# Moving the loads of three attention units inside a fused kernel

## The chip, the cores and the metric

The kernel runs on one core of one Trainium2 chip. The metric is the device time of one execution in microseconds (us). Before the change it is 703.27 us, the median of three runs (702.09 to 704.14).

## The reference

The reference is a chain of three blocks on a batch of 4, with 8 heads, 768 positions and a head size of 48:

```
f = sigmoid(f_logit)                                  # gated linear attention, token by token
state = f_t * state + k_t (outer) v_t ;  y_t = q_t . state
x = y, heads side by side                             # [4, 768, 384]
h = relu(x^T @ w_tok1) @ w_tok2 ; u = x + h^T         # mixer over tokens (256 hidden)
x2 = u + relu(u @ w_ch1) @ w_ch2                      # mixer over channels (1536 hidden)
h = relu(x2 @ w_in)                                   # gated feed-forward (1024 hidden)
out = (h * sigmoid(conv3(h))) @ w_out                 # conv of 3 taps along the sequence
```

Weights arrive as 64-bit floats.

## The kernel before, in words

The attention is cut into 16 **units**: unit u is one batch and one pair of heads, so units 0 to 3 are batch 0. A unit has four inputs, `f`, `k`, `q` (112 x 768 each) and `v` (128 x 6 x 96). `elem_steps(u)` turns the forget gates into decay factors: s1 to s3 on ScalarE (L385, L388, L391: exp, then log in two halves), s4 a running sum on VectorE (L396), s5 a small copy (L401) and exp on ScalarE (L403), s7 multiplies `k` by it (L410), s6 is another exp on ScalarE (L406) and s8 multiplies `q` by that (L414). For units 0 to 4 both products run on VectorE. Then TensorE transposes `k` (`T`), multiplies chunks of `q` and `k` (`A`), sums up states (`U`) and forms the output (`Y`). ScalarE copies their results out, L468 (`am`), L420 (`kn` and the states `S`), L521 (`xn`); GpSimd masks `am` (L469).

The weights are cut into 34 pieces (0 to 33). Each is loaded into a staging buffer (L318), decoded from 64-bit by three VectorE operations (L65, L67, L69) and split into a high part on ScalarE (L329) and a low part on VectorE (L330). The first 20 pieces have six staging buffers by turns; two decoded buffers exist, so a decode waits until the piece two before it is split.

The kernel has four stretches: the **front** (`first_gla`, units 0 to 3, with the decode of the first pieces woven in); then for each batch an MLP of token and channel mixer (`mlp_a`), into which the units of the next batch are woven (`gla_steps`, `merge`); last the gated feed-forward of all batches. The first MLP also decodes the late weight pieces.

What sets the order: every matrix multiplication, every first operation of a decode (L65) and the steps of units 1 and 4 to 15 are kept in the order of the code. All else (DMA issues on the queue of SyncE, ScalarE, the rest of VectorE) is put in order by a planner that runs a timeline of its own: at each moment an engine is given, of the instructions that its model holds ready, the one that stands first in the code. An instruction is ready when its inputs are there and its buffer has been given up by the last reader. The order is then fixed; on the chip every engine works through its list and waits at the head of it.

Loads are issued in SyncE's queue by `load_unit(u)` (f, k, q) and `load_v(u)`. Their buffers: `f` one (tag "f", pool `gl`), but units 1 and 3 share another ("r10", pool `pa`); `k` two; `q` three, but unit 3 takes one of the four buffers "xhl" that later hold the split of x; `v` two. In the code, step u of the front ends with the loads of unit u+2 (`load_unit(u + 2)`, `load_v(u + 2)`), and so do the steps in `gla_steps`. `zipl` weaves two lists evenly.

Of the kernel before, what the change touches and what calls it, by code (L numbers as in the profile page):

```python
# [8 lines left out]
F32 = mybir.dt.float32  # L9
# [9 lines left out]
B, H, S, D = 4, 8, 768, 48  # L19
DM = H * D  # L20
NP_ = H // 2
P = 128
DT_TOK, D_CH, D_FF = 256, 1536, 1024
HR = 112
# [196 lines left out]
def chunked_path(ctx, tc, psum, flags, qT, kT, fT, vN, w_tok1, w_tok2, w_ch1, w_ch2, w_in, conv_w, w_out, outT):  # L221
    nc = tc.nc
# [42 lines left out]
    pa = ctx.enter_context(tc.tile_pool(name="pa", bufs=1))  # L265
    gl = sa.enter_context(tc.tile_pool(name="gl", bufs=2))

    units = [(b, p) for b in range(B) for p in range(NP_)]
    st = [dict() for _ in units]

    def load_unit(u, between=(lambda: None,) * 3):
        b, p = units[u]
        d = st[u]
        pool, tag = (pa, "r10") if u in (1, 3) else (gl, "f")
        d["f"] = pool.tile([HR, S], F32, tag=tag, name=f"f{u}", bufs=1)
        d["k"] = gl.tile([HR, S], F32, tag="k", name=f"k{u}")
        if u == 3:
            d["q"] = pa.tile([HR, S], F32, tag="xhl", name=f"q{u}", bufs=4)
        else:
            d["q"] = gl.tile([HR, S], F32, tag="q", name=f"q{u}", bufs=3)  # L280
        for i, (n, src) in enumerate((("f", fT), ("k", kT), ("q", qT))):
            nc.sync.dma_start(out=d[n], in_=src[b, p])
            between[i]()

    def load_v(u):
        b, p = units[u]
        st[u]["v"] = gl.tile([P, NC_, 2 * D], F32, tag="v", name=f"v{u}")
        nc.sync.dma_start(out=st[u]["v"], in_=vN[b, p])
# [21 lines left out]
    def weight_piece(dst, src, n, shape, pool, stage=("wst", 3)):  # L310

        cols = shape[0] * (shape[1] if len(shape) > 1 else 1)
        box = {}

        def load():
            box["s"] = pool.tile([P, cols], I64, tag=stage[0], name=f"wst{n}", bufs=stage[1])
            o = box["s"]
            nc.sync.dma_start(out=o if len(shape) == 1 else o.rearrange("p (a b) -> p a b", a=shape[0]), in_=src)  # L318

        def dec():  # L320
            box["w"] = pool.tile([P, cols], U32, tag="wdc", name=f"wdc{n}", bufs=2)

            decode_f64(nc, box["w"], box["s"], tc.keep_in_program_order)
            w = box["w"].bitcast(F32)
            box["w"] = w if len(shape) == 1 else w.rearrange("p (a b) -> p a b", a=shape[0])

        def split():
            ready.add(n)
            nc.scalar.activation(dst[0], box["w"], AF.Copy)  # L329
            (nc.vector if isinstance(n, int) else nc.gpsimd).tensor_tensor(  # L330
                out=dst[1], in0=box["w"], in1=dst[0].bitcast(F32), op=ALU.subtract)

        return [load, dec, split]

    def pipelined(pieces, lead=1):
        res = []
        n = len(pieces)
        for i in range(n + lead + 1):
            g = []
            if 0 <= i - lead < n:  # L340
                g.append(pieces[i - lead][1])
            if 0 <= i - lead - 1 < n:
                g.append(pieces[i - lead - 1][2])
            if i < n:
                g.append(pieces[i][0])
            res.append(g)
        return res
# [17 lines left out]
    first = [f for g in wgroups[:LEAD] for f in g]  # L365
    wgroups = wgroups[LEAD:]
    first[0]()
    load_unit(1, (first[1], lambda: load_v(0), first[2]))
    wlate = pipelined([weight_piece(d, sr, NDEEP + n, sh, pa) for n, (d, sr, sh) in enumerate(wpieces[NDEEP:])], LATE)

    def conv_weights():
# [7 lines left out]
    def elem_steps(u):  # L379
        d = st[u]  # L380

        pin = tc.keep_in_program_order if u >= NP_ or u == 1 else lambda ins: ins

        def s1():
            pin(nc.scalar.activation(d["f"], d["f"], AF.Exp, scale=-1.0, accum_out=SE[:, u:u + 1]))  # L385

        def s2():
            pin(nc.scalar.activation(d["f"][:, :HS], d["f"][:, :HS], AF.Ln, bias=1.0, accum_out=T1[:, u:u + 1]))  # L388

        def s3():  # L390
            pin(nc.scalar.activation(d["f"][:, HS:], d["f"][:, HS:], AF.Ln, bias=1.0))  # L391

        def s4():
            pool, tag = (pa, "r11") if u in (1, 3) else (gl, "c")
            d["c"] = pool.tile([HR, S], F32, tag=tag, name=f"c{u}", bufs=1)
            (pin if u != 1 else lambda ins: ins)(nc.vector.tensor_tensor_scan(d["c"], zcol[:HR].to_broadcast([HR, S]), d["f"], T1[:, u:u + 1],  # L396
                                                                 op0=ALU.add, op1=ALU.subtract))

        def s5():

            pin(nc.vector.tensor_scalar(out=T2[:, u:u + 1], in0=d["c"][:, S - 1:S], scalar1=-1.0, scalar2=None,  # L401
                                        op0=ALU.mult))
            pin(nc.scalar.activation(d["f"], d["c"], AF.Exp, scale=-1.0))  # L403

        def s6():
            pin(nc.scalar.activation(d["c"], d["c"], AF.Exp))  # L406

        def s7():
            eng = nc.vector if KE[min(u, 5)] == "v" else nc.gpsimd
            eng.tensor_tensor(out=d["k"], in0=d["k"], in1=d["f"], op=ALU.mult)  # L410

        def s8():
            eng = nc.vector if QE[min(u, 5)] == "v" else nc.gpsimd
            eng.tensor_tensor(out=d["q"], in0=d["q"], in1=d["c"], op=ALU.mult)  # L414

        return [s1, s2, s3, s4, s5, s7, s6, s8]
# [13 lines left out]
    def pm(*a, **k):  # L430

        tc.keep_in_program_order(mm(*a, **k))  # L432
# [93 lines left out]
    def new_x(b):  # L526
        xn[b] = pa.tile([P, NC_, DM], F32, tag="xn", name=f"xn{b}", bufs=2)

    def first_gla(wb):

        def keep_busy(u):

            for _ in range(NBUSY[u]):
                pm(wb[:, :256], lhsT=wz[:, :P], rhs=wz, start=True, stop=True)

        e = elem_steps(1)
        parts = [elem_steps(0) + e[:3] + [lambda: load_v(1), lambda: new_x(0)]]
        for u in range(NP_ + 1):
            ahead, products = [], []
            if u + 1 < NP_:  # L540
                ahead = elem_steps(u + 1) if u else e[3:]
                if u + 2 < NP_ + 1:
                    ahead += [lambda u=u: load_unit(u + 2), lambda u=u: load_v(u + 2)]
            if u < NP_:
                products += [lambda u=u: T(u), lambda u=u: A(u, 0), lambda u=u: A(u, 1)]
            if u:
                products += [lambda u=u: Y(u - 1, 0), lambda u=u: Y(u - 1, 1)]
            if u < NP_:
                products += [lambda u=u: U(u)]
            parts.append(zipl([joined(f, lambda u=u: keep_busy(u)) for f in products], ahead))  # L550
        return sum(parts[:4], []), sum(parts[4:], [])

    def gla_steps(b):

        u0, n = b * NP_, (b + 1) * NP_
        steps = []
        for u in range(u0 if b == 1 else u0 + 1, n + 1):
            new = u < len(units)
            s = []
            if new:  # L560
                s.append([lambda u=u: T(u)])
            s.append([lambda u=u: A(u, 0)] * new + [lambda u=u: Y(u - 1, 0)] * (u > u0))
            s.append([lambda u=u: A(u, 1)] * new + [lambda u=u: Y(u - 1, 1)] * (u > u0))
            if b == 1 and u == u0:

                s.append([])
            s[-1] += [lambda u=u: U(u)] * new
            ahead = []
            if u + 1 < len(units):
                ahead = elem_steps(u + 1)  # L570
            if u + 2 < len(units):
                ahead += [lambda u=u: load_unit(u + 2), lambda u=u: load_v(u + 2)]
            if u + 1 == n and n < len(units):
                ahead = [lambda: new_x(b + 1)] + ahead

            cuts = [0, 4, 7 if b == 1 else 6] if len(s) > 2 else [0, 4]
            for i, blk in enumerate(s):
                steps.append(joined(*blk))
                steps += ahead[cuts[min(i, len(cuts) - 1)] if i < len(cuts) else len(ahead):
                               cuts[i + 1] if i + 1 < len(cuts) else len(ahead)]  # L580
        return steps

    def joined(*fs):
        return lambda: [f() for f in fs]
# [298 lines left out]
    for i in range(len(seq) + 2):  # L883
        if i < len(seq):
            b, ff = seq[i]
# [6 lines left out]
            for _ in range(min(len(wsteps), 2)):  # L892
                f = wsteps.pop(0)
# [54 lines left out]
```

## Time and profile before

| | |
|---|---|
| median of 3 runs | 703.27 us |
| the profiled execution's own time | 702.62 us |
| its span, first to last instruction | 700.9 us |
| PE busy | 680.8 us (97%) |
| DVE (VectorE) busy | 407.0 us (58%) |
| ACT (ScalarE) busy | 292.1 us (42%) |
| POOL (GpSimd) busy | 116.5 us (17%) |
| moved by DMA | 55.19 MB |

The span is counted from the first to the last instruction. The engines' shares are means over stretches with different limits: TensorE is nearly always busy after the front, while in the front, the first 57.5 us, several engines and the DMA engines have their turns as the limit.

### The profile page before, as it was taken

The numbers are of one execution on the slowest core, as the hardware profiler recorded it, in microseconds if no ns is written. First come the engines' busy times: TensorE is split into PE (matmuls) and PEld (weight loads), VectorE is DVE, ScalarE is ACT, GpSimd is POOL, SyncE is SP. The second block draws the span as 40 slices with busy tenths as digits, with TensorE's granted clock in tenths as the row PEclk, the third lists the DMA queues.
The fourth block names the chain that finished last, engine by engine and source line by source line (L and its number), as shares of the span: only waits on it lengthen the run. The fifth ranks groups of instructions, "written<-read, shape, count | busy, mean of one in ns | idle before, by whom it ended". The sixth has DMA issues, their size and how long they took to land.

```text
span 700.9 us, 12681 instructions
## 1 busy us (share of the span) xinstructions
PE 680.8 (97%) x5228; PEld 651.8 (93%) x5228; DVE 407.0 (58%) x719; ACT 292.1 (42%) x613; POOL 116.5 (17%) x96
## 2 busy tenths in 40 slices
PE   7898999999999999999999999999999999999995
PEld 5678998999999999999999999999999999999995
DVE  6799995554334432143342154384677968876774
ACT  6665355554433342233234132242444544444432
POOL 2340002234112113011112022332303004000000
PEclk9979999999999999999999999999999999999999
DMA  9995453244022302002001021240301200100102
GB/s 238 267 265 163 141 177 93 78 119 112 35 77 77 91 21 77 35 20 59 35 19 68 20 83 69 79 158 23 102 0 49 88 1 0 68 1 1 68 0 73
DMA packets 26114, 55.19 MB, mean 79 GB/s; under 512 B 2880, under 2 KB 12096, under 8 KB 26048
## 3 DMA queue, kind: packets, MB, share of 16 engines
q1 hardware_dynamic: 22448, 49.38, 23.9%
q10 hardware_dynamic: 3600, 4.92, 2.0%
q8 instruction: 43, 0.70, 0.4%
q14 instruction: 23, 0.19, 0.1%
HBM read 44.85 MB, written 9.44 MB: 77 GB/s over the span
## 4 chain that ended last, share of the span: by engine, by line
PE 79%; DVE 7%; DMA 6%; issue 3%; ACT 2%; POOL 1%; SPq 0%; ACTq 0%; POOLq 0%; DVEq 0%
PE acc L432 22%; PE c L432 19%; PE h L844 14%; PE o L866 13%; PE Y L432 4%; PE t L432 4%; DMA f<-in_fT_dram 4%; PE A L432 3%; DVE wdc L67 1%; DMA wst<-in_w_tok_dram 1%; DVE wdc L69 1%; DMA x2d<-xo 1%; DVE wdc L65 1%; DVE c L396 1%; DVE wc L330 1%
## 5 line engine op out<-in xcount | busy, mean ns | idle before, releaser
L432 PE MATMUL c<-u,wc 128*128 128x384 f32 x864 | 169.4, 339 | 0.8 <-ACT u L671 0.4
L432 PE MATMUL acc<-hid,wc 128*128 128x384 f32 x864 | 164.6, 336 | 0.0
L432 PEld LDWEIGHTS c<-u,wc 128*128 128x128 f32 x864 | 149.5, 188 | 5.7 <-DVE u L672 1.6
L432 PEld LDWEIGHTS acc<-hid,wc 128*128 128x128 f32 x864 | 150.5, 188 | 0.5
L646 DVE SCALAR_TENSOR_TENSOR hid<-c,hid 128x384 fp32r<-128x384 f32 x96 | 53.4, 556 | 135.7 <-ACT hid L645 135.4
L844 PE MATMUL h<-x2r,wi 128*128 128x384 f32 (+2 forms) x576 | 108.9, 338 | 0.1
L866 PE MATMUL o<-gbuf,wo 128*128 128x384 f32 x576 | 105.8, 335 | 0.0
L844 PEld LDWEIGHTS h<-x2r,wi 128*128 128x128 f32 x576 | 101.6, 188 | 0.4 <-ACT hp L846 0.4
L866 PEld LDWEIGHTS o<-gbuf,wo 128*128 128x128 f32 x576 | 100.5, 188 | 0.4 <-ACT gbuf L827 0.4
L645 ACT ACTIVATE hid<-c 128x384 fp32r<-128x384 f32 x96 | 47.0, 490 | 118.2 <-PE c L432 117.8
L823 DVE SCALAR_TENSOR_TENSOR cv<-hp,cwu,cv 128x768 f32<-128x768 f32 (+1 forms) x66 | 69.8, 1058 | 1.2
L825 ACT ACTIVATE cv<-cv 128x768 f32<-128x768 f32 (+1 forms) x33 | 27.3, 827 | 69.2 <-DVE cv L823 69.0
L410 POOL TENSOR_TENSOR k<-k,f 112x768 f32<-112x768 f32 x11 | 20.1, 1826 | 181.7 <-ACT f L403 101.0
L826 DVE TENSOR_TENSOR cv<-cv,hp 128x768 f32<-128x768 f32 (+1 forms) x33 | 32.5, 983 | 25.5 <-ACT cv L825 25.4
L846 ACT ACTIVATE hp<-h 128x384 f32<-128x384 f32 (+1 forms) x64 | 30.6, 485 | 26.7 <-PE h L844 26.5
L784 POOL TENSOR_TENSOR x2r<-x,x2r 128x768 fp32r<-128x768 f32 x12 | 24.7, 2080 | 94.8 <-ACT x2r L783 86.2
L828 DVE TENSOR_TENSOR gbuf<-cv,gbuf 128x768 fp32r<-128x768 f32 (+1 forms) x33 | 32.3, 979 | 5.4 <-ACT gbuf L827 5.3
L396 DVE TENSOR_TENSOR_SCAN c<-zcol,T,f 112x768 f32<-112x768 f32 x16 | 29.0, 1813 | 9.5 <-ACT f L391 9.5
L432 PEld LDWEIGHTS A<-q,k 48*128 48x128 f32 x384 | 25.7, 194 | 9.5 <-issue 5.5
L432 PE MATMUL A<-q,k 48*128 48x128 f32 x384 | 32.4, 298 | 1.2 <-DVE am L472 0.4
L827 ACT ACTIVATE gbuf<-cv 128x768 fp32r<-128x768 f32 (+1 forms) x33 | 27.2, 823 | 15.2 <-DVE cv L826 12.6
L821 DVE TENSOR_SCALAR cv<-hp,cwu 128x768 f32<-128x768 f32 (+1 forms) x33 | 23.1, 699 | 15.7 <-ACT hp L846 15.6
(97 smaller groups left out, 737.3 us busy)
## 6 DMA issues: line engine op xcount, KB each, us to landing
wst<-in_w_ch_dram SPq DMA_DIRECT2D x24, 384.0 KB, 3.6
f<-in_fT_dram SPq DMA_DIRECT2D x16, 336.0 KB, 4.5
k<-in_kT_dram SPq DMA_DIRECT2D x16, 336.0 KB, 4.0
q<-in_qT_dram SPq DMA_DIRECT2D x16, 336.0 KB, 5.8
v<-in_vN_dram SPq DMA_DIRECT2D x16, 288.0 KB, 5.1
x2d<-xo ACTq DMA_DIRECT2D x24, 192.0 KB, 1.9
x<-x2d SPq DMA_DIRECT2D x8, 576.0 KB, 4.5
out_dram<-ot SPq DMA_DIRECT2D x23, 192.0 KB, 2.0
```

The source lines that it names most:

```text
L396: (pin if u != 1 else lambda ins: ins)(nc.vector.tensor_tensor_scan(d["c"], zcol[:HR].to_broadcast([HR, S]), d["f"], T1[:, u:u + 1], op0=A ...
L432: tc.keep_in_program_order(mm(*a, **k))
L645: nc.scalar.activation(dst[:, 0, :], src, AF.Relu)
L646: nc.vector.scalar_tensor_tensor(out=dst[:, 1, :], in0=src, scalar=0.0, in1=dst[:, 0, :].bitcast(F32), op0=ALU.max, op1=ALU.subtract)
L823: nc.vector.scalar_tensor_tensor(out=t[:, c], in0=h[:, lo + i:hi + i], scalar=cw[:, ff, i:i + 1], in1=t[:, c], op0=ALU.mult, op1=ALU.add)
L825: nc.scalar.activation(t[:, c], t[:, c], AF.Sigmoid)
L826: nc.vector.tensor_tensor(out=t[:, c], in0=t[:, c], in1=h[:, lo + 1:hi + 1], op=ALU.mult)
L827: nc.scalar.activation(gg[:, 0, c], t[:, c], AF.Copy)
L828: nc.vector.tensor_tensor(out=gg[:, 1, c], in0=t[:, c], in1=gg[:, 0, c].bitcast(F32), op=ALU.subtract)
L844: mm(ps, lhsT=w[a], rhs=x2["r", b][c][:, k, lo:hi], start=(i == 0), stop=(i == 8))
L846: nc.scalar.activation(h[:, 1 + lo:1 + hi], ps, AF.Relu)
L866: mm(o, lhsT=w[a], rhs=gg[:, c, hf * HS:(hf + 1) * HS], start=(ff == 0 and a == 0 and c == 0), stop=(ff == NFF - 1 and c == 1))
```

## The change

`load_part(u, n)` loads one of a unit's inputs. Unit 2's `f` gets a buffer of the tag "xhl" and stands in the code behind unit 1's `q` and before unit 0's `v`. Unit 2's `q` stands behind unit 1's `v`; its `k` behind unit 3's `f`, at the end of step 0. Unit 3's `q` and `k` and unit 2's `v` end step 1, unit 3's `v` step 2. Unit 4's four loads are moved from step 2 to the last step of the front. In the later batches `load_v(u + 1)` stands where `load_v(u + 2)` stood. No computation changes.

```diff
+    def load_part(u, n):
+        b, p = units[u]
+        d = st[u]
+        if n == "f":
+            pool, tag, bufs = (pa, "r10", 1) if u == 3 else (pa, "xhl", 4)
+        elif n == "k":
+            pool, tag, bufs = gl, "k", 2
+        else:
+            pool, tag, bufs = (pa, "xhl", 4) if u == 3 else (gl, "q", 3)
+        d[n] = pool.tile([HR, S], F32, tag=tag, name=f"{n}{u}", bufs=bufs)
+        nc.sync.dma_start(out=d[n], in_={"f": fT, "k": kT, "q": qT}[n][b, p])
...
     first[0]()
-    load_unit(1, (first[1], lambda: load_v(0), first[2]))
+    load_unit(1, (first[1], lambda: None, lambda: load_part(2, "f")))
+    load_v(0)
+    first[2]()
...
-        parts = [elem_steps(0) + e[:3] + [lambda: load_v(1), lambda: new_x(0)]]
+        parts = [elem_steps(0) + e[:3] + [lambda: load_v(1), lambda: load_part(2, "q"), lambda: new_x(0)]]
...
                 ahead = elem_steps(u + 1) if u else e[3:]
-                if u + 2 < NP_ + 1:
-                    ahead += [lambda u=u: load_unit(u + 2), lambda u=u: load_v(u + 2)]
+            if u == 0:
+                ahead += [lambda: load_part(3, "f"), lambda: load_part(2, "k")]
+            elif u == 1:
+                ahead += [lambda: load_part(3, "q"), lambda: load_part(3, "k"), lambda: load_v(2)]
+            elif u == 2:
+                ahead += [lambda: load_v(3)]
+            elif u == 4:
+                ahead += [lambda: load_v(4), lambda: load_unit(4)]
...
             if u + 2 < len(units):
-                ahead += [lambda u=u: load_unit(u + 2), lambda u=u: load_v(u + 2)]
+                ahead += [lambda u=u: load_unit(u + 2)]
+            if u0 < u < len(units) - 1:
+                ahead += [lambda u=u: load_v(u + 1)]
```

## Rows read from the trace of the kernel before

**Rows 1.** Windows view, three stretches; busy us (instructions) of each engine, clock, DMA share, GB/s

```profile
20.00:25.00 5.00, 5.00 (x94) 3.94 (x94) 1.10 (x3) 2.41 (x7) 0.97 (x2) 1.00 1.05 283
25.00:57.50 32.50, 26.74 (x363) 20.19 (x359) 31.45 (x58) 23.09 (x61) 11.29 (x12) 0.82 0.97 268
57.50:95.00 37.50, 37.50 (x212) 36.98 (x213) 35.21 (x81) 16.14 (x34) 0.00 (x0) 0.98 0.46 142
```

**Rows 2.** Chain of waits, 0 to 110 us; start us, length us, what

```profile
18.85 10.21 DMA f<-in_fT_dram
...
95.08 0.48 DVE wc L330
...
95.60 0.61 PE c L432 x2
```

**Rows 3.** Timeline of ACT; start us, length us, operation [idle before <- what ended it]

```profile
22.57 0.84 ACT L385 ACTIVATE f<-f 112x768 f32<-112x768 f32 x1 [3.67 <-DMA f<-in_fT_dram]
...
29.09 0.84 ACT L385 ACTIVATE f<-f 112x768 f32<-112x768 f32 x1 [0.77 <-DMA f<-in_fT_dram]
```

**Rows 4.** Timeline of DVE, 9 to 32 us

```profile
9.06 0.96 DVE L410 TENSOR_TENSOR k<-k,f 112x768 f32<-112x768 f32 x1 [0.72 <-ACT f L403]
...
24.44 0.43 DVE L330 TENSOR_TENSOR wt<-wdc,wt 128x256 fp32r<-128x256 f32 x1 [3.73 <-ACT wt L329]
25.35 1.82 DVE L396 TENSOR_TENSOR_SCAN c<-zcol,T,f 112x768 f32<-112x768 f32 x1 [0.49 <-ACT f L391]
27.09 0.40 DVE L330 TENSOR_TENSOR wt<-wdc,wt 128x256 fp32r<-128x256 f32 x1
...
27.47 0.66 DVE L65 TENSOR_SCALAR wdc<-wst 128x256 uint32<-128x256 uint32 x1
28.16 0.73 DVE L67 SCALAR_TENSOR_TENSOR wdc<-wst,wdc 128x256 uint32<-128x256 uint32 x1
28.93 0.51 DVE L69 SCALAR_TENSOR_TENSOR wdc<-wst,wdc 128x256 uint32<-128x256 uint32 x1
29.36 1.15 DVE L410 TENSOR_TENSOR k<-k,f 112x768 f32<-112x768 f32 x1
30.79 0.96 DVE L414 TENSOR_TENSOR q<-q,c 112x768 f32<-112x768 f32 x1 [0.28 <-ACT c L406]
```

**Rows 5.** Timeline of SyncE's queue, 0 to 60 us; DMA issues

```profile
5.14 0.71 SPq L282 DMA_DIRECT2D q<-in_qT_dram  x1
...
14.22 0.33 SPq L282 DMA_DIRECT2D f<-in_fT_dram  x1
...
17.66 0.33 SPq L282 DMA_DIRECT2D k<-in_kT_dram  x1
...
46.33 0.33 SPq L282 DMA_DIRECT2D k<-in_kT_dram  x1
```

**Rows 6.** View of tile q, around 5.2 us: issue to landing

```profile
DMA to landing us min/median/max: 10.2/10.2/10.2
```

**Rows 7.** View of tile f, around 14.25 us: issue to landing

```profile
DMA to landing us min/median/max: 8.3/8.3/8.3
```

**Rows 8.** View of tile k, around 17.7 us: issue to landing

```profile
DMA to landing us min/median/max: 10.1/10.1/10.1
```

**Rows 9.** Timeline of PE, 16 to 57 us

```profile
16.68 1.43 PE L432 MATMUL A<-v,kn 128*48 128x240 f32 x20 [2.63 <-ACT am L468]
...
30.66 0.67 PE L432 MATMUL T<-perm,k 112*128 112x112 f32 x5 [1.76 <-DVE k L410]
...
45.55 0.71 PE L432 MATMUL A<-q,k 48*128 48x128 f32 x8
...
54.44 0.55 PE L432 MATMUL Y<-S,q 112*64 112x96 f32 x8 [2.59 <-ACT S L420]
```

**Rows 10.** The page's part 6; load, KB each, median us from issue to landing

```profile
f<-in_fT_dram SPq DMA_DIRECT2D x16, 336.0 KB, 4.5
...
v<-in_vN_dram SPq DMA_DIRECT2D x16, 288.0 KB, 5.1
```

## The prediction, made before the changed kernel was run

> **What bounds the kernel now.** I read the 40 slices of the page first, then windows of the first 100 us, the chain of waits, and the timelines of ACT, DVE, SyncE's queue and PE. After 95 us PE is the limit and hardly idles, so a change of load order can matter only before. In the windows [rows 1] the reader is to see three things. The DMA engines are full (share 1.05, then 0.97) up to 57.5 us. DVE is nearly idle from 20 to 25 us (1.10 us busy of 5) and nearly full after it: 31.45 of 32.5, 35.21 of 37.5. And PE, which looks busy, waits at the points that matter: 1.76 us for the product k of unit 2, 2.59 us for the copy of unit 3's states [rows 9]. The chain [rows 2] runs from a landing of `f` at 29.06 (18.85 + 10.21) through DVE work up to 95.56, where PE waits for the split of a weight piece. So from about 29 to 95 us DVE's throughput is the limit, and a microsecond is won for the whole kernel only if DVE gets work done earlier in its idle stretch.
>
> That stretch has a plain cause. ACT stands 3.67 us at s1 of unit 2 until its `f` lands at 22.5 [rows 3]; the split of a piece stands behind it, DVE waits 3.73 us for that split and 0.49 us more for unit 2's s3 [rows 4]: 4.2 us, the most that the change can win here.
>
> **Part by part.**
>
> *f of unit 2 in front.* It was the 16th load in the queue, issued at 14.22 and landed 8.3 us later, at 22.5 [rows 5, 7]. Now it is the 9th. The 9th load so far (unit 1's `q`) was issued at 5.14 and landed at 15.3 [rows 5, 6]; one load of 336 KB [rows 10] in place of unit 0's `v` of 288 KB before it adds some 0.2 us. So `f` lands at about 15.5, 7 us sooner, and ACT's 3.67 us are gone. DVE can start the running sum about where its idle time began, 24.44 - 3.73 = 20.7, end it at 22.5, and go on with what the list has between it and the product: two splits 0.43 + 0.40, and the decode of piece 4, 0.66 + 0.73 + 0.51, together 2.73 us [rows 4]. That is done at about 25.3.
>
> *What is late next: k of unit 2.* The product L410 started at 29.36 [rows 4], but its `k` landed only at 17.66 + 10.1 = 27.8 [rows 5, 8]. It was the 20th load, behind pieces 6 and 7, because its buffer is given up by A of unit 0. The change moves it in the code, not in what it waits for. If it keeps its place, the product begins at 27.8: 1.6 us sooner, and DVE idles from 25.3 to 27.8. Most of the 4.2 us is then not won but moved.
>
> *Unit 4's loads at the end of the front.* In the code they stand last; in the queue I expect three of them where they were. Loads of units far down the code are already issued as soon as a buffer is free: `k` of unit 5 at 46.33, when the last A of unit 3 ended at 45.55 + 0.71 = 46.26 [rows 5, 9]. Unit 4's `q`, `k`, `v` wait for Y of unit 0, A of unit 2 and Y of unit 2 in both kernels, so they cost nothing either way; the time from there to unit 4's steps, well inside the first MLP, hides them. But its `f` loses its wait: the buffer "f" is now free when the product of unit 0 ends, at 9.06 + 0.96 = 10.0 [rows 4], just what unit 2's `f` used to wait for before it was issued at 14.22. By the planner's rule unit 4's `f`, useless for a long while, takes about that place, at latest in the first moment when nothing else is ready. Then as many loads as before, plus one, stand ahead of `k` of unit 2 and `f` of unit 3. The price of one: the 16th load landed at 22.5 and the 21st, five later, at 29.06 [rows 2, 5, 7], so 1.3 us. `k` of unit 2 lands at 29.1, its product begins 29.36 - 29.1 = 0.3 us sooner than now. That is my value. The bounds: -1.6 us (unit 4's `f` behind both), and +1.2 us if besides ACT's list keeps s1 of unit 3 ahead of L406 of unit 2, as it does now (s1 at 29.09 [rows 3], and the product of `q` at 30.79 waiting for L406 [rows 4]): s1 then waits until 30.3 instead of 29.06, and L406 and that product wait with it. I take -0.3 since L406 can be ready some us earlier than now.
>
> The Trainium skill, "DMA: Bandwidth & Descriptors", section Specifications, gives about 358 GB/s of HBM for one core. By it a load of 336 KB would be an estimated 0.96 us, and the sum here -0.6 in place of -0.3. The trace differs: 283 and 268 GB/s with the DMA engines full [rows 1], and I go by the landings.
>
> *v of unit 0 and pieces 2 to 5.* Each goes back by one load, 1.3 us at most. U of unit 0 started at 16.68 [rows 9]; its `v` now lands near 16.6. It costs 0 to 0.3 us there, and ACT may stand up to 3 us at s1 of unit 2 if the planner's model has `f` landed sooner than 15.5. Both fall in the time before 29 us in which DVE waits for `k` anyway; without that cover they would cost their length.
>
> *v a unit later.* The buffer of v(u+1) is given up by Y(u-1), in the same step, whether the load stands early or late in the code. Cost nothing: PE's work of a whole step hides it; uncovered it would be one landing, 5.1 us [rows 10], once.
>
> *The sum.* On the profiled execution 702.62 - 0.3 = 702.3. It lies 0.65 below the median, and the changed kernel's time is a median too, so I give 703.27 - 0.3 = 703.0.
>
> **Rivals.**
>
> 1. *Unit 4's `f` stays behind `k` of unit 2* (the queue is never without a readier load). For: loads are taken in code order when several are ready. Against: `k` (early in the code) went out behind pieces 6 and 7, so the queue had moments in which `k` wasn't ready and `f` would be. Gain 1.6: 701.7.
> 2. *DVE fills the wait.* The product of `q` (0.96) and the decode of piece 5 (as piece 4: 0.66 + 0.73 + 0.51 = 1.9) stand before the product of `k`; both inputs are there. Then 0.3 + 0.96 + 1.9 = 3.2 us are won: 700.1; the full 4.2 would be 699.1. For: L406 needs only the running sum. Against: piece 5 stands behind `k`'s product in the code, and a decode needs the piece two before it split.
> 3. *Slower: DVE's list has the product of `k` ahead of the 2.73 us of splits and decode*, since the planner sees `f` so early and `k` landing far sooner than 27.8. Then DVE stands at it with that work undone, and all of it comes after 29.1: 2.73 - 0.3 = 2.4 us later: 705.7. It decides at the operation that stands before L65 of piece 4. Against: those operations stand earlier in the code than the product.
>
> The change doing half of what it says (unit 4's loads not at the end) is in the forecast.
>
> **How the numbers follow.** A run can tell 0.3%, 2.1 us, from no change. Forecast (-1.0 to +1.2 us): 0.38, with 702.3 to 704.5 of its own. Rival 1: 0.15, same. Rival 2: 0.27, faster. Rival 3: 0.20, slower, though a tenth of it stays under 2.1. With 0.02 of rival 1 going past 2.1: faster 0.29, same 0.38 + 0.13 + 0.02 = 0.53, slower 0.18. The range takes in rival 2 to 3.7 of its 4.2 us and rival 3 with 0.2 us on top: 699.6 to 705.9.
>
> **What would show it.** In the changed profile: unit 2's `f` as the 9th load, landing near 15.5, and no wait of ACT for it near 22; a load of `f` between 14 and 19 us that nobody reads until the first MLP; DVE idle before L410 of unit 2, ended by a DMA of `k` at 28 to 29; T of unit 2 at 30.4; the start of the token mixer (57.5) within 1 us of now. Wrong: T of unit 2 before 28, or a token mixer that starts over 2 us from 57.5 either way.

## The result and the profile after

The changed kernel is slower. Its median is 707.72 us (706.33 to 709.10, 10 runs); the kernel before, on the same chip, has 704.09 us (702.09 to 707.03, 10 runs). The ratio is 1.0056, 95% interval 1.0041 to 1.0072. The prediction was 703.0 us with a range up to 705.9 and "within 0.3%" as the likeliest case: the measured time lies above the range, and the case that came, slower, had the lowest of the three chances, 0.18.

The profiled execution took 708.30 us, its span 706.6. The first part of its page gives busy time, share and instructions of each engine; PE's and DVE's sums are within 2 us of before: of the 5.7 us by which the span grew, PE's busy time took 1.5, the rest is waiting.

```profile
PE 682.3 (97%) x5228; PEld 652.5 (92%) x5228; DVE 407.2 (58%) x719; ACT 291.4 (41%) x613; POOL 113.0 (16%) x96
```

The early part came nearly as foretold. SyncE's queue (start us, length us; L296 is the new `load_part`, L282 `load_unit`): unit 2's `f` at 4.80, unit 4's `f` at 15.58, unit 2's `k` at 18.29.

```profile
4.80 0.49 SPq L296 DMA_DIRECT2D f<-in_fT_dram  x1
...
15.58 0.33 SPq L282 DMA_DIRECT2D f<-in_fT_dram  x1
18.29 0.33 SPq L296 DMA_DIRECT2D k<-in_kT_dram  x1
```

Unit 2's `f` is the 9th load and lands 10.0 us later, at 14.8 instead of 22.5 [rows 7]. Unit 4's `f`, which nobody reads until the first MLP, went out in front of unit 2's `k`, though it stands last in the code of the front; `k` landed 11.4 us after its issue, at 29.7, which answers to [rows 8].

Timelines of ACT, DVE and PE, the instructions that answer to [rows 3], [rows 4] and [rows 9] (in brackets the idle time before and what ended it).

```profile
14.85 0.84 ACT L400 ACTIVATE f<-f 112x768 f32<-112x768 f32 x1 [2.86 <-DMA f<-in_fT_dram]
30.92 0.84 ACT L400 ACTIVATE f<-f 112x768 f32<-112x768 f32 x1 [3.36 <-DMA f<-in_fT_dram]
```

```profile
17.04 1.82 DVE L411 TENSOR_TENSOR_SCAN c<-zcol,T,f 112x768 f32<-112x768 f32 x1 [0.43 <-ACT f L406]
...
29.75 0.96 DVE L425 TENSOR_TENSOR k<-k,f 112x768 f32<-112x768 f32 x1 [3.28 <-DMA k<-in_kT_dram]
```

```profile
19.33 2.64 PE L447 MATMUL A<-v,kn 128*48 128x240 f32 x20 [5.09 <-ACT am L483]
...
33.99 0.64 PE L447 MATMUL T<-perm,k 112*128 112x112 f32 x5
...
55.53 0.55 PE L447 MATMUL Y<-S,q 112*64 112x96 f32 x8 [0.99 <-ACT S L435]
```

The wait at s1 of unit 2 has moved from 22.6 to 14.9 us; DVE then waits 3.28 us for `k`. PE pays for the early wait (5.09 us before U of unit 0) and T of unit 2 is 3.3 us late, but the token mixer starts at 58.00, 0.5 us later than before, and the channel mixer's first transposes at 64.39, 0.3 us earlier than before. Up to there nothing is lost.

The loss is made in the **first half of the first channel mixer**. The windows view answers to the last of [rows 1] and goes on to 105 us; below it is the same stretch of the kernel before, which isn't among the rows shown.

```profile
57.50:95.00 37.50, 36.80 (x214) 35.69 (x210) 35.10 (x80) 16.48 (x36) 0.00 (x0) 1.00 0.46 134
95.00:105.00 10.00, 8.26 (x34) 7.36 (x35) 8.86 (x23) 4.85 (x12) 0.00 (x0) 0.83 0.51 158
```

```profile
95.00:105.00 10.00, 9.93 (x57) 9.61 (x57) 10.00 (x23) 6.20 (x13) 0.00 (x0) 1.00 0.55 167
```

Timeline of PE from 92 us, the changed kernel:

```profile
92.67 1.72 PE L447 MATMUL acc<-hid,wc 128*128 128x384 f32 x9
94.23 0.34 PE L447 MATMUL c<-u,wc 128*128 128x384 f32 x1
95.00 1.48 PE L447 MATMUL c<-u,wc 128*128 128x384 f32 x5 [0.43 <-DVE wc L343]
97.62 0.45 PE L447 MATMUL c<-u,wc 128*128 128x384 f32 x1 [1.14 <-ACT wc L342]
98.59 0.61 PE L447 MATMUL c<-u,wc 128*128 128x384 f32 x2 [0.53 <-DVE wc L343]
99.05 2.47 PE L447 MATMUL acc<-hid,wc 128*128 128x384 f32 x9
101.31 2.60 PE L447 MATMUL c<-u,wc 128*128 128x384 f32 x9
103.75 1.55 PE L447 MATMUL acc<-hid,wc 128*128 128x384 f32 x8
```

A group of nine matmuls, from one start to the next, takes 1.56 us (92.67 to 94.23). The group at 94.23 takes until 99.05: 4.82, so 3.26 us too many, with three waits for pieces of the weight `wc` (2.10 us in all; the other 1.16 lie in the four parts that the group falls into, which together last longer than nine matmuls in a row). The two groups behind it take 2.26 and 2.44 instead of 1.56: 1.58 more, with the granted clock between the two levels, 1.2 and 2.4 GHz (mean 0.64 from 99.05 to 103.75). Sum 4.8 us. The first half as a whole is 4.88 us longer than before. That the two figures are so near is partly luck: the kernel before also loses 0.5 us at this group (2.08 us, 93.97 to 96.05), and the changed kernel had lost about as much in the groups ahead of it. The second half of the channel mixer starts 4.6 us later than before, the last instruction ends 5.7 us later; the 1.1 us between the two are no more than two executions of one kernel differ there (e14).

Why the pieces are late is seen in DVE's timeline. L65 is the first step of a decode, L646 (before) and L670 (after) the split of a `hid` tile, which waits for PE. Before:

```profile
87.34 0.55 DVE L646 SCALAR_TENSOR_TENSOR hid<-c,hid 128x384 fp32r<-128x384 f32 x1
87.81 0.35 DVE L65 TENSOR_SCALAR wdc<-wst 128x384 uint32<-128x384 uint32 x1
...
90.08 0.55 DVE L646 SCALAR_TENSOR_TENSOR hid<-c,hid 128x384 fp32r<-128x384 f32 x1
90.55 0.35 DVE L65 TENSOR_SCALAR wdc<-wst 128x384 uint32<-128x384 uint32 x1
...
91.91 0.36 DVE L65 TENSOR_SCALAR wdc<-wst 128x384 uint32<-128x384 uint32 x1
```

After:

```profile
87.16 0.56 DVE L670 SCALAR_TENSOR_TENSOR hid<-c,hid 128x384 fp32r<-128x384 f32 x1
...
90.30 0.56 DVE L670 SCALAR_TENSOR_TENSOR hid<-c,hid 128x384 fp32r<-128x384 f32 x1 [0.59 <-ACT hid L669]
90.78 0.35 DVE L65 TENSOR_SCALAR wdc<-wst 128x384 uint32<-128x384 uint32 x1
...
93.45 0.56 DVE L670 SCALAR_TENSOR_TENSOR hid<-c,hid 128x384 fp32r<-128x384 f32 x1 [0.18 <-ACT hid L669]
...
94.97 0.36 DVE L65 TENSOR_SCALAR wdc<-wst 128x384 uint32<-128x384 uint32 x1
```

The decodes at 87.81 and 91.91 are those of pieces 28 and 30. In the changed kernel they begin at 90.78 and 94.97, each behind a hid split that DVE had to wait for. The lists of the two kernels, decodes as w and hid splits as h(0), h(1), ... (low splits of weights left out):

```
before: w25 w26 h(5) w27 h(6) w28 h(7) w29 w30 h(8) w31 w32 h(9) w33 h(10)
after:  w25 h(5) w26 w27 h(6) h(7) w28 w29 h(8) w30 w31 w32 w33 h(9)
```

Pieces 28 and 30 stand behind h(7) and h(8) instead of h(6) and h(7). A hid split needs PE's group before it, and PE's next groups need the pieces: DVE can't be ahead with them. The lists differ ahead of w25 too, from the decode of piece 15 on, but between 57 and 113 us these three waits are the only ones of PE.

### The profile page after: what moved, and what is told of

It reads as the page before. It is cut to its first block, busy times and chain, and to the rows that moved or that the text cites. A ratio compares the mean times of both kernels' runs of the same rounds, so it can differ in the third digit from the quotient of the medians.

```text
span 706.6 us, 12683 instructions
## 1 busy us (share of the span) xinstructions
PE 682.3 (97%) x5228; PEld 652.5 (92%) x5228; DVE 407.2 (58%) x719; ACT 291.4 (41%) x613; POOL 113.0 (16%) x96
## 4 chain that ended last, share of the span: by engine, by line
PE 84%; DVE 6%; DMA 5%; ACT 3%; issue 2%; POOL 0%; SPq 0%; ACTq 0%; DVEq 0%; POOLq 0%
PE acc L447 24%; PE c L447 21%; PE h L868 14%; PE o L890 14%; PE Y L447 4%; PE t L447 3%; PE A L447 3%; DMA k<-in_kT_dram 2%; DMA f<-in_fT_dram 2%; DMA v<-in_vN_dram 1%; DVE wdc L67 1%; DVE wdc L69 1%; DVE c L411 1%; PE T L447 1%; DVE wdc L65 1%
## 5 line engine op out<-in xcount | busy, mean ns | idle before, releaser
L447 PE MATMUL c<-u,wc 128*128 128x384 f32 x864 | 172.2, 343 | 2.7 <-ACT wc L342 1.1
L447 PEld LDWEIGHTS c<-u,wc 128*128 128x128 f32 x864 | 151.8, 189 | 8.2 <-DVE wc L343 1.9
L670 DVE SCALAR_TENSOR_TENSOR hid<-c,hid 128x384 fp32r<-128x384 f32 x96 | 53.4, 556 | 132.1 <-ACT hid L669 131.6
L411 DVE TENSOR_TENSOR_SCAN c<-zcol,T,f 112x768 f32<-112x768 f32 x16 | 29.1, 1817 | 15.3 <-ACT f L406 15.3
L487 DVE TENSOR_TENSOR am<-A,cmask 128x512 f32<-128x512 f32 (+1 forms) x48 | 25.1, 552 | 12.1 <-PE A L447 10.0
```

Source lines behind the costliest of these rows:

```text
L670: nc.vector.scalar_tensor_tensor(out=dst[:, 1, :], in0=src, scalar=0.0, in1=dst[:, 0, :].bitcast(F32), op0=ALU.max, op1=ALU.subtract)
```

## The experiments

Three theories. **A**: DVE is late, because x's first split now stands ahead of the decode of piece 15, and the delay reaches the pieces of 95 us. **B**: the early front is the loss (ACT's stand at 14.9, PE's gap at 19, unit 4's `f` in front of `k`). **C**, formed on e4: neither delay, but the order in which DVE's list alternates decodes and hid splits.

This table holds what I read from PE's timeline of each profile: the first matmul of the token mixer; the length of the first half of the first channel mixer, from its first transposes (`acc<-ident,xn`) to those of the second half; and the end of the last instruction. Ratios are to the kernel before measured beside each kernel, with 95% intervals. Its median was 702.91 us for e1 to e4, 704.47 for e5 to e8, 703.27 for e9 to e12 and 703.60 for e13, so medians of different groups are not to be compared.

| kernel | token mixer at | first half takes | end | median us | ratio |
|---|---|---|---|---|---|
| before | 57.48 | 42.32 | 700.92 | 704.09 | |
| before, second profile (e14) | 58.51 | 42.33 | 704.27 | | |
| after | 58.00 | 47.20 | 706.60 | 707.72 | 1.0056 [1.0041, 1.0072] |
| e1 unit 4's loads at the end | 58.23 | 47.02 | 706.69 | 708.54 | 1.0079 [1.0054, 1.0104] |
| e2 f of unit 2 alone | 56.89 | 43.97 | 702.99 | 704.73 | 1.0027 [1.0008, 1.0046] |
| e3 seven empty entries | 58.29 | 43.51 | 703.80 | 707.48 | 1.0076 [1.0051, 1.0102] |
| e4 ACT's unit 2 in order | 55.90 | 47.21 | 704.72 | 706.95 | 1.0069 [1.0044, 1.0094] |
| e5 after, hid splits pinned | 55.98 | 43.91 | 702.51 | 706.22 | 1.0022 [1.0003, 1.0042] |
| e6 e1, hid splits pinned | 57.32 | 43.67 | 702.82 | 704.92 | 1.0017 [1.0001, 1.0033] |
| e7 v a unit later alone | 57.12 | 42.32 | 702.25 | 704.06 | 0.9999 [0.9981, 1.0017] |
| e8 candidate | 56.68 | 42.55 | 702.08 | 704.56 | 1.0011 [0.9995, 1.0027] |
| e9 before, two empty entries | 57.77 | 45.86 | 705.77 | 707.62 | 1.0061 [1.0044, 1.0078] |
| e10 after, no new entries | 59.96 | 43.60 | 708.87 | 707.93 | 1.0057 [1.0035, 1.0080] |
| e11 candidate | 57.46 | 43.91 | 703.78 | 704.32 | 1.0016 [1.0001, 1.0030] |
| e12 candidate | 57.78 | 42.56 | 704.23 | 704.81 | 1.0015 [0.9995, 1.0034] |
| e13 e1, no new entries | 56.92 | 42.36 | 703.20 | 704.49 | 1.0004 [0.9982, 1.0025] |

The first halves follow DVE's list. From piece 20 on, the kernels of this table have three orders of decodes and hid splits. Where the order is that of before (before twice, e7, e8, e12, e13), the first half takes 42.3 to 42.6 us; where pins force this order (e5, e6, e11), 43.7 to 43.9. Where it is the changed kernel's (after, e1, e4, e9), it takes 45.9 to 47.2 (the 1.3 us between them are taken up in the last section). A third order, in e2, e3 and e10, gives 43.5 to 44.0:

```
third:  w25 h(4) w26 w27 h(5) w28 h(6) w29 h(7) w30 w31 h(8) w32 w33 h(9) h(10)
```

### e1: one part of the change alone

```diff
-                if u + 2 < NP_ + 1:
+                if u + 2 < NP_:
...
+            if u == 4:
+                ahead += [lambda: load_v(4), lambda: load_unit(4)]
```

> The kernel before with one part of the change alone: unit 4's four loads stand in the last step of the front; unit 2's f, and v, as before. The loads themselves go out in nearly the same order; but the weave of that last step has more entries, so the code has the split of x ahead of the decode of piece 15, and VectorE's list follows. Theory A (the loss is made there: VectorE waits for the split of x with the decode of piece 15 behind it, all later pieces are late, and TensorE stalls for the last of them between 90 and 100 us): 2 to 5 us slower than the kernel before, so about 706 to 709, VectorE idle for 1 to 2.5 us before the first split of x, TensorE waiting 1 to 2.5 us for split weight pieces near 95 us. Theory B (the loss is made early: ScalarE stands at unit 2's s1, TensorE's gap of 5 us follows, unit 4's f is in front of unit 2's k): none of this is in this kernel, so within 1 us of the kernel before.

Measured 708.54 us: this part, which I had priced at nothing, costs as much as the whole change. Its front is nearly that of before up to piece 14 (the loads and DVE's list differ by a swap); then x's split stands ahead of piece 15, and PE's three waits are those of the changed kernel, at 95.48, 98.11 and 99.08 us (0.43, 1.14, 0.53). Theory B falls: there is no early wait in this kernel.

### e2: the other part alone

```diff
...
-    load_unit(1, (first[1], lambda: load_v(0), first[2]))
+    load_unit(1, (first[1], lambda: None, lambda: load_part(2, "f")))
+    load_v(0)
+    first[2]()
...
-                    ahead += [lambda u=u: load_unit(u + 2), lambda u=u: load_v(u + 2)]
+                    ahead += [lambda u=u: load_unit(u + 2)] if u else [lambda: load_part(2, "k"), lambda: load_part(2, "q")]
+                    ahead += [lambda u=u: load_v(u + 2)]
```

> The kernel before with unit 2's f alone moved: in a buffer of its own, loaded in front of unit 0's v. ScalarE's early stand at s1 of unit 2, the gap of TensorE near 15 us and unit 4's f ahead of unit 2's k are all in it; the decode of piece 15 stays ahead of the split of x. Theory A: within 1.5 us of the kernel before (702.5 to 705.5), since VectorE works off as much by the end of the front. Theory B: as slow as the changed kernel, 706 to 709.

Measured 704.73, ratio 1.0027. It has ACT's early wait and PE's gap, and unit 4's `f` in front as well, and starts the token mixer 0.6 us sooner than before. By the ratios that is half of the change's 0.56%; the interval excludes 1, but only just. The long stall isn't in it, but its first half is 1.65 us longer than before: this edit, too, changed the list (the third order).

### e3: piece 15 ahead of x's split again

```diff
-              zipl(rest + xpre(0), sum(wgroups[NFIRST:], []))):
+              zipl(rest + [lambda: None] * 7 + xpre(0), sum(wgroups[NFIRST:], []))):
```

> The changed kernel with seven empty entries in the last weave ahead of the split of x, which put the decode of piece 15 (and 16, 17 one place each) ahead of the split of x in VectorE's list; all loads as in the changed kernel. Theory A: the 3 to 4 us come back, 702.5 to 705, VectorE idle under 1 us before the first split of x. Theory B: as the changed kernel, 706 to 709.

The median lies in B's range (706 to 709), not in A's, and it says against C that the long stall can go and the time stay. In the profile the three waits are gone but for 0.2 us and the first half takes 43.51 (the third order, not that of before); that execution was the fastest of six (705.51). The other five took 706.89 to 709.85, and what they lost no trace shows.

### e4: the early wait taken away

```diff
-        pin = tc.keep_in_program_order if u >= NP_ or u == 1 else lambda ins: ins
+        pin = tc.keep_in_program_order if u >= NP_ or u in (1, 2) else lambda ins: ins
```

> The changed kernel with ScalarE's steps of unit 2 kept in the order of the code, so that s1 of unit 2 comes after unit 1's states and ScalarE no longer stands at it near 12 us; the split of x still stands ahead of the decode of piece 15. Theory A: the gap of TensorE near 15 us goes (5.1 to under 3 us), yet the time stays 2 us or more above the kernel before, 705.5 to 709. Theory B: 2 to 4 us faster than the changed kernel, 703 to 705.5.

The early wait is gone and the token mixer starts 1.6 us earlier than before, at 55.90. PE's waits are the same, 1.6 us sooner than in the changed kernel:

```profile
93.43 1.48 PE L447 MATMUL c<-u,wc 128*128 128x384 f32 x5 [0.43 <-DVE wc L343]
96.05 0.44 PE L447 MATMUL c<-u,wc 128*128 128x384 f32 x1 [1.14 <-ACT wc L342]
97.03 0.62 PE L447 MATMUL c<-u,wc 128*128 128x384 f32 x2 [0.53 <-DVE wc L343]
```

Theory B falls again: without the early wait, and with 2.06 us in place of PE's 5.09, the kernel is as slow. Theory A says that lateness makes the waits; here all is 1.6 us earlier and they are equal to 0.01 us. A fixed order does that: DVE waits for PE (hid), PE for DVE (the piece), whenever they get there. So theory C. This run alone doesn't decide between A and C, since x's split still stands ahead of piece 15 and PE is earlier by as much; e5 and e6 do.

### e5 and e6: the order pinned, nothing else

```diff
+    dec_of = {}
+    BEHIND = {0: 20, 1: 21, 2: 22, 3: 23, 4: 24, 5: 26, 6: 27, 7: 28, 8: 30, 9: 32, 10: 33}
...
-            decode_f64(nc, box["w"], box["s"], tc.keep_in_program_order)
+            dec_of[n] = decode_f64(nc, box["w"], box["s"], tc.keep_in_program_order)
...
-                relu_split(hd, o)
+                with tc.issue_after(dec_of[BEHIND[ft]].ins) if (b, hf) == (0, 0) and ft in BEHIND else ExitStack():
+                    relu_split(hd, o)
```

`decode_f64` now returns the first operation of a decode. The pin holds both halves of a hid split, ScalarE's and VectorE's, so the order of ScalarE's list changes with it.

> The changed kernel with one thing pinned: in the first half of the first channel mixer each split of a hid tile (VectorE's lines L646 and L670) is held behind the decode of the weight piece that it stands behind in the kernel before, so that pieces 28 and 30 no longer stand behind the hid splits 7 and 8. The first split of x still stands ahead of the decode of piece 15, and the early front is the changed kernel's own. Theory A (the loss is VectorE being late, because x's split stands ahead of piece 15): PE's stalls between 93 and 99 us stay, the second half of the first channel mixer starts 4 to 5 us later than before, 706 to 709 us. Theory C (the loss is the order in which VectorE's list alternates decodes and hid splits): the three stalls and the low granted clock behind them go, the second half starts at most 1.5 us later than before, 703 to 705.5 us.

> The kernel before with unit 4's loads at the end of the front (which by itself measured 5.6 us slower) and the same pins of the hid splits behind the decodes. Theory C: what is left is the late start of the token mixer (0.75 us), so 703 to 705 us, at most 1.5 us above the kernel before of the same chip. Theory A: the loss stays, 706 to 709 us.

The three waits are gone in both. The windows view from 90 to 105 us, the changed kernel and then e5:

```profile
90.00:105.00 15.00, 12.83 (x61) 11.61 (x60) 13.35 (x33) 6.93 (x16) 0.00 (x0) 0.89 0.54 172
```

```profile
90.00:105.00 15.00, 14.93 (x85) 14.39 (x84) 14.75 (x32) 8.08 (x17) 0.00 (x0) 1.00 0.56 167
```

PE does 85 instead of 61 of its matmuls in these 15 us. e6 measured what C gave (704.92); e5's profiled execution, 704.22, lies in C's range too, but its median of 706.22 lies at the low end of A's (706 to 709). The kernel before had measured 704.09 and 702.91 when those ranges were written; beside e5 it took 704.47, and the ratio fell from 1.0056 to 1.0022. What A said of the stalls failed in both kernels: they are gone although x's split still stands ahead of piece 15. So A falls, and the order of decodes and hid splits makes the stalls. Both first halves are still 1.3 to 1.6 us longer than before: the pins make a wait of their own, of 0.7 us, at the first hid split (at 71.07 us in e5).

### e7: v a unit later alone

```diff
-                ahead += [lambda u=u: load_unit(u + 2), lambda u=u: load_v(u + 2)]
+                ahead += [lambda u=u: load_unit(u + 2)]
+            if u0 < u < len(units) - 1:
+                ahead += [lambda u=u: load_v(u + 1)]
```

> The kernel before with only v's load a unit later in the later batches; front and first MLP as before. All theories, A, B and C: nothing, within 1 us of the kernel before. If it is 2 us or more slower, part of the loss belongs to this edit and the theories lack it.

Nothing, 0.9999.

### e9: the order made worse, with nothing moved

```diff
+            if u == 4:
+                ahead += [lambda: None] * 2
```

> The kernel before with two entries that do nothing put where the change puts unit 4's two loads; every load stays in its place, and no instruction is added, taken away or changed. VectorE's list of the first MLP comes out as in the kernel that had unit 4's loads moved (x's split ahead of piece 15, pieces 28 and 30 behind one hid split more). Theory C (the order of that list is the whole loss): PE stalls of about 0.4, 1.1 and 0.5 us between 93 and 100 us, the second half of the first channel mixer 4 to 5 us later than before, 706.5 to 709.5 us, as slow as the change. Theory B, and any theory in which a load in another place costs the time: nothing, within 1.5 us of the kernel before.

The decisive run. Every load stands where it stood, and two functions that do nothing make the kernel as slow as the change, 707.62. PE's timeline:

```profile
95.48 1.48 PE L432 MATMUL c<-u,wc 128*128 128x384 f32 x5 [0.43 <-DVE wc L330]
98.11 0.44 PE L432 MATMUL c<-u,wc 128*128 128x384 f32 x1 [1.15 <-ACT wc L329]
99.08 0.61 PE L432 MATMUL c<-u,wc 128*128 128x384 f32 x2 [0.53 <-DVE wc L330]
99.53 1.75 PE L432 MATMUL acc<-hid,wc 128*128 128x384 f32 x9
101.12 1.72 PE L432 MATMUL c<-u,wc 128*128 128x384 f32 x9
102.68 1.72 PE L432 MATMUL acc<-hid,wc 128*128 128x384 f32 x9
```

In the trace the lists of PE, GpSimd and SyncE's queue are those of the kernel before, by operation and tile from first to last; ScalarE's and VectorE's are not, and ScalarE's is that of e1.

`zipl` spreads the weights' steps evenly over the entries of the other list. Two entries more, empty or not, shift each weight step against the splits of x in the code; the planner, which goes by the place in the code, then makes another list for DVE and ACT. It takes effect at 95 us, though the edit is in the last step of the front, before 58 us. How the planner gets from the one to the other I did not trace.

### e10 and e13: unit 4's loads at the end without entries of their own

The edit of e10 against the changed kernel; e13 has the same last two lines in the kernel before, with the loads taken out of step 2 as in e1.

```diff
-            elif u == 4:
-                ahead += [lambda: load_v(4), lambda: load_unit(4)]
...
+            if u == 4:
+                parts[-1][-1] = joined(parts[-1][-1], lambda: load_v(4), lambda: load_unit(4))
```

> The changed kernel with unit 4's two loads still at the end of the front, but called from the last entry that was there already, so that the last weave has as many entries as before; nothing is pinned. In VectorE's list piece 15 stands ahead of x's split again, and pieces 28 and 30 behind seven and eight hid splits or fewer. Theory C: no stall near 95 us, second half of the first channel mixer at most 2 us later than before, 703.5 to 706 us: what f of unit 2 alone measured (704.7). Theory B (the early front is the loss, and its order is the changed kernel's own): 706.5 to 709.

> The kernel before with unit 4's two loads at the end of the front, called from the entry that was the last one of the last weave, so that the number of entries stays what it was; VectorE's list of the first MLP then has the order of the kernel before. With two entries of their own the same loads measured 5.6 us. Theory C (what costs is the two entries, by the order they give VectorE's list): within 1.5 us of the kernel before, no stall of PE between 93 and 100 us, second half of the first channel mixer within 1.5 us of before. If the place of the loads costs something by itself: 706 us or more.

e13 is clean: in the kernel before, the loads at the end cost nothing (1.0004) as long as they don't count as entries, and the first half takes 42.36. e10 missed: the long stall is gone, as C said, and the kernel is as slow as the change all the same. With unit 2's `f` in front the list has the third order, and the first half takes 1.28 us more than before, with 0.2 and 0.3 us left of PE's waits. The token mixer starts late, at 59.96. PE waits 3.00 us ahead of it, for the copy of unit 3's states; in ScalarE's list a weight's split stands in front of that copy, and the split waits for a decode. Timelines of ACT and PE:

```profile
54.91 0.52 ACT L342 ACTIVATE wc<-wdc 128x384 fp32r<-128x384 f32 x1 [1.48 <-DVE wdc L69]
```

```profile
56.13 0.58 PE L447 MATMUL Y<-S,q 112*64 112x96 f32 x8 [3.00 <-ACT S L435]
```

This doesn't explain the loss, for the kernel before does the same: it waits 2.59 us there [rows 9], 3.06 in its second profile, behind the same split:

```profile
53.22 0.52 ACT L329 ACTIVATE wc<-wdc 128x384 fp32r<-128x384 f32 x1 [1.62 <-DVE wdc L69]
```

The profiled execution is also the slowest of the four (710.66; the fastest two took 706.45 and 706.62). e3, which has the same lists but for VectorE's around x's first splits, is as slow (707.48); e2, with the third order as well, isn't (704.73). So C explains the stall of the changed kernel and its cost, but not every slow kernel here: what e3 and e10 lose beyond 1.2 to 1.3 us in the first half stays open.

### e14: the kernel before once more

> The kernel before once more, unchanged, for a second profile of it. If the 0.8 us that every kernel tried loses between 112 and 183 us, and up to 1.2 us more behind, belong to the edits, this profile has its token mixer of batch 1 within 0.3 us of 177.4 us and its end within 0.5 us of 700.9. If they are what one execution differs from another, the transfers of the first 15 us (247 GB/s from 5 to 10 us in the profile at hand, 267 to 285 in others) and these markers differ by 1 us or more between two profiles of one kernel.

The second profile of the same kernel ends 3.35 us later, and its token mixer of batch 1 starts at 180.37 instead of 177.39. From the second half (109.21) to there it takes 71.16 us, in the first profile 70.39: the 0.8 us, with no edit at all. In two stretches of its windows view the granted clock (third from the end) and the GB/s (last) count:

```profile
5.00:10.00 5.00, 3.98 (x37) 3.33 (x34) 2.68 (x3) 3.05 (x7) 0.00 (x0) 1.00 1.04 271
57.50:64.00 6.50, 6.35 (x29) 5.86 (x26) 4.38 (x10) 2.90 (x7) 0.00 (x0) 0.59 0.44 139
```

The token mixer took 66.88 - 58.51 = 8.37 us, with a clock of 0.59 from 57.5 to 64 us; in the first profile 64.68 - 57.48 = 7.20, with 0.86. So 1 to 3 us in the start of the token mixer or in the end say nothing between two single profiles; the length of the first half (42.32 and 42.33) does.

### e8, e11, e12: versions meant to beat both

e8 is e4 with the seven empty entries of e3, unit 4's loads called from one entry, and its `f`, `k` and `q` held behind unit 3's `k`; e11 is e4 with the pins of e5; e12 is e4 with the loads joined to the last entry as in e10.

> A candidate for a version faster than both: the changed kernel with ScalarE's steps of unit 2 kept in the order of the code, unit 4's loads held behind the load of unit 3's k in SP's queue, and seven empty entries ahead of x's split in the last weave, by which the decode of piece 15 goes back ahead of it and the hid splits stand behind the decodes as in the kernel before. Theory C: the token mixer starts 1 to 2 us earlier than before and no stall stands near 95 us, so 700.5 to 703 us. Theory B (each microsecond of the early front is kept): the same, and more the earlier the token mixer starts. Theory A: 702 to 704. If what is won by 58 us is taken back before 112 us, 703 us or more, whatever the list.

> A candidate: the changed kernel with ScalarE's steps of unit 2 in the order of the code and the hid splits pinned behind the decodes as in the kernel before. Without the pins it started the token mixer 1.6 us earlier than before and measured 706.9 us. Theory C: the pins take the 3 to 4 us at 93 to 105 us away, so 702 to 704.5 us. If what is won by 58 us were kept to the end it would be 702; the run with the pins alone kept about half of it to 107 us and none that can be seen at the end, so 703.5 is the likelier.

> The other way to the same order, with no pins on the hid splits: ScalarE's steps of unit 2 in the order of the code, unit 4's loads called from the last entry that was there, by which piece 15 also goes ahead of x's split. Theory C: no stall near 95 us, 702 to 704.5 us, within 1 us of the run with the pins. If piece 15 ahead of x's split costs the token mixer's start what it saves later, about 704.

All three are rid of the loss (704.56, 704.32, 704.81) and none is faster than before. e8 missed its range (700.5 to 703), e12 by 0.3 us; e11 is in it. e12 has the order of before and a first half nearly as short (42.56), with unit 2's `f` in front, so what is left of the change without its side effect, and with ScalarE's unit 2 in order, is 1.0015 [0.9995, 1.0034], no difference that was measured.

## Why the prediction was wrong

- **f of unit 2 in front**: right. 9th load, landed at 14.8 (said 15.5), ACT's 3.67 us at 22.6 gone, the running sum even at 17.04 (said 20.7), as the planner now puts it ahead of piece 2.
- **k of unit 2 is late next; unit 4's f goes out in front of it**: right. `k` landed at 29.7 (said 29.1), the product began at 29.75, 0.4 us later than before and not 0.3 us sooner. T of unit 2, said for 30.4, came at 33.99: I had taken it to follow the product, but PE had U of unit 1 ahead of it, at 32.18 us. U waited 1.02 us for ACT's copy of `am`, which stood in ACT's list behind s1 of unit 3 and its wait of 3.36 us for `f`. The prediction had that wait only as a bound, and only for L406 and the product of `q`.
- **v of unit 0 one load later, ACT up to 3 us at s1**: ACT waited 2.86. "Both fall in the time before 29 us" held for DVE, not for PE (5.09 us before U), and the token mixer's start shows that it cost nothing much all the same: 58.00, within the 1 us said.
- **Unit 4's loads "cost nothing either way"**: this is the step that failed. I put `q`, `k` and `v` at nothing and `f` at one load, all as transfers, and as transfers they do cost nothing (e13, 1.0004). They were also two entries of a list that is woven evenly with the decode of the weights, and two such entries cost 0.61% by themselves (e9), 0.44 to 0.78: DVE's and ACT's lists come out in another order, and PE stands three times near 95 us. The sum had no term for the order of the lists.
- **"A change of load order can matter only before" 95 us**: the chain [rows 2] had ended in a DVE split at 95.08 that PE waited for at 95.60, so the pieces there had no slack at all. I used this row for DVE's throughput up to 95 us and not for what it says of the order there. Nor is the chain DVE work all the way from 29 us: from 54.44 to 72.30 it runs on PE, and later for 4 us on a weight's landing, so "DVE's throughput is the limit" was too strong.

```profile
57.48 7.36 PE t L432 x36
...
79.25 4.06 DMA wst<-in_w_ch_dram
```

- **Rival 3**, the slower one, named the right kind of thing, a place in DVE's list, at the wrong place (unit 2's product of `k`) and at half the price. The forecast's gain of 0.3 us was too small to be tested.

What the early front gains or loses is not settled. Of the seven kernels with `f` of unit 2 in front and without the long stall, five (e2, e5, e8, e11, e12) measured 0.1 to 0.3% above before, and two (e3, e10) 0.6 to 0.8%, for a reason that stays open. Of the five, e2, e5 and e11 have first halves 1.6 us too long, e8 and e12 don't, and their intervals include no change.

## What to carry to other kernels

Where a planner fixes the order of engines from the order of the code, an edit has two prices: that of its instructions, and that of the lists it changes elsewhere. Compare the compiled lists of every engine before and after, not only the moved instructions; and test the second price by itself, with an edit that changes the list and nothing else. Two engines that wait for each other in turn (PE for a decoded piece, DVE for a `hid` tile) can make a stall of fixed size from a few places swapped in a list, and starting earlier didn't shorten it here (e4).

## What the runs showed that I had not expected

The clock's answer to one stall differs. After the same three waits, equal within 0.02 us, the changed kernel ran its next two groups at a granted clock of 0.64 and took 4.70 us; in e9 the clock stayed at 1.00, the same groups took 102.68 - 99.53 = 3.15 us, and the first half was 1.3 us shorter (45.86 against 47.20). Windows of the changed kernel, then of e9 (granted clock third from the end):

```profile
99.00:101.30 2.30, 2.30 (x11) 2.30 (x10) 1.91 (x7) 1.40 (x4) 0.00 (x0) 0.67 0.14 44
101.30:103.75 2.45, 2.45 (x11) 2.45 (x11) 1.93 (x5) 1.83 (x5) 0.00 (x0) 0.61 0.54 157
```

```profile
99.00:102.00 3.00, 2.92 (x17) 2.92 (x18) 2.38 (x8) 2.29 (x7) 0.00 (x0) 1.00 0.32 117
```

The Trainium skill, "TensorE: Matmul & The Clock Gate", section "What's actually happening", says that how many matmuls run slow at a kernel's start varies from run to run. Here two executions of one kernel, the kernel before, differ in the middle: granted clock 0.86 and 0.59 from 57.5 to 64 us (e14).

The first loads don't come at one rate. Between 5 and 10 us, with the DMA engines full, the two profiles of the kernel before moved 247 and 271 GB/s. The changed kernel and e5 have the same first loads and landed unit 2's `k` at 29.66 and 27.64 us; e5 started its token mixer 2.0 us sooner.
